# Two transposes taken from TensorE and done by VectorE in 32x32 blocks and by DMA through DRAM, in a fused local/pooled attention and maxout kernel

## The chip, the cores and the metric

The kernel runs on one core of a Trainium2 chip. The core has five engines that run at once: TensorE (PE in the profile), VectorE (DVE), ScalarE (ACT), GpSimd (POOL) and SyncE (SP, which here only issues DMA transfers). The metric is the device time of one execution in microseconds (us); lower is better.

## The reference

Two kinds of attention over 8 batches x 8 heads x 576 tokens x 64 dims are added, and the sum goes through a maxout layer. All is float32.

```python
q_d = q.reshape(B, H, Sd, factor, D).mean(axis=3)        # factor = 4, Sd = 144; k_d and v_d alike
out_up = np.repeat(sm_attn(q_d, k_d, v_d), factor, axis=2)   # pooled attention, full softmax over 144
mask = np.abs(pos[:, None] - pos[None, :]) < factor       # local attention: 7 neighbours
scores = np.where(mask, scale * np.matmul(q, k.transpose(0, 1, 3, 2)), -1000000000.0)
attn = softmax(scores)
x = (out_up + np.matmul(attn, v))                         # then (8 * 576, 512)
h = np.maximum(np.maximum(x @ w1, x @ w2), x @ w3)        # 512 -> 768
return h @ w_out                                          # 768 -> 512
```

## The kernel before, in words

The 4608 tokens are cut into nine blocks `j` of 512 tokens. Block `j` from 0 to 7 is the first 512 tokens of batch `j`; block 8 collects the last 64 tokens of all eight batches. In a block, token `4r + f` lies in partition `r` at position `f`, so that one partition holds a pooled group of four tokens. A block's attention runs in two halves `n = 2j` and `n = 2j + 1` of four heads each.

**Local attention of blocks 2 to 8.** `scores(n)` computes windows of scores on TensorE, writes them to DRAM (`scr`) and reads them back so that each token's seven scores lie in its partition (`s`). `values(n)` loads V with its neighbours (`v`, two buffers), multiplies it by the seven weights into `pvb` (on ACT, POOL or DVE) and adds up on DVE into `x`, a tile of 128 partitions (r) x 4 (f) x 128 (two heads x 64 dims). Each block has four such tiles, `c = 0..3`; tag `x` has five buffers. Blocks 0 and 1 take another path (`DENSE`, `band_values`) that leaves x already transposed.

**Pooled attention of blocks 0 to 7.** `pooled_scores(n)` multiplies pooled q and k on TensorE, takes maxima on DVE, exponentials on ACT (into `pd`, 128 x 2 x 2 x 144, and the tail's `pdt`, 64 x 144), and then needs the softmax with the key on the partition. Before, TensorE transposes it with the identity: four matmuls of `pd`, one of `pdt`, one of `ptl`, and a small one of `ptd` with `diag` that gathers the corner; copies bring the results from PSUM into `pt` and `ptt`. `pooled_values(n)` multiplies them by pooled V (`vd`, `vtail`) and ACT scales the result into `od`.

**The maxout layer** (`mlp_in`, `mlp_out`) needs x with the feature on the partition. `turn(j)` calls `transposes(j, c)`: before, four TensorE transposes of an x tile into one PSUM bank (`psx`), one DVE add of `od` into `xs` (tag `t`, three buffers), and a split into a high part `xhi` (ACT) and a low part `xlo`. The float32 product is made of three products of high and low parts, so a block costs 216 matmuls in `mlp_in` (tile names `xhi`, `xlo`, `whi`, `wlo`) and 72 in `mlp_out` (`hh`, `wo`), each 128x128 by 512 columns. `xhi` and `xlo` have one buffer for each `c`, so block `j + 1` can be split only when `mlp_in(j)` has read them.

**What sets the order.** The kernel's code only records operations. A planner in it (`Recorder.place`) gives each operation a cost, a priority and a readiness time, runs a list schedule with these costs and writes every engine's instructions in that order; where an operation has several forms (`either`, `copy`, `tt`) it also picks the engine. On the chip each engine then executes its list in order, and waits where an operand has not come. Transfers are all issued by SP in such a list. On PE, attention comes before the maxout layer whenever it is ready by the plan, and the maxout layer fills the rest. Since one helper emits everything, all instructions carry one line in the profile (L409); they are told apart by their tiles. PSUM has eight banks, four of tag `pm` for the maxout layer (and block 0), four of tag `pa`.

Of the kernel before, what the change touches and what calls it, by code (L numbers as in the profile page):

```python
# [28 lines left out]
HH = 4  # L29
# [7 lines left out]
SCR = HH * SEG * (KWIN + 1)  # L37
QKW = S + 6
# [73 lines left out]
class Recorder:  # L112
# [46 lines left out]
    def add(self, forms, bias={}):  # L159
# [20 lines left out]
        for write, aps in ((False, ins), (True, outs)):  # L180
            for ap in aps:
# [245 lines left out]
def local_global_attention_maxout_kernel(ctx: ExitStack, tc: tile.TileContext, qk_d, qke_d, vw_d, wi_d, wo_d, v, ident_d, mask_d, diag_d, band_d, out):  # L427
# [47 lines left out]
    pdt = new([P, SD], name="pdt")  # L475
# [37 lines left out]
    def load_constants():  # L513
        for t in (*qtail, *vtail, pdt, ptd, ptl, nm, zd):
            dve.memset(t, 0.0)
# [61 lines left out]
    def tail_pooled(n):  # L577
# [7 lines left out]
        vs = new([N64, D], tag="vs", name=f"vs_{n}")  # L585
# [3 lines left out]
    def pooled_scores(n):  # L589
# [15 lines left out]
        pd = new([P, 2, 2, SD], tag="pd", name=f"pd_{n}")  # L605
        for x in range(4):
            i, pr = x // 2, x % 2
            act.activation(pd[:, i, pr], sps[i][:, pr], AF.Exp, bias=nm[:, x : x + 1], scale=1.0 / 128.0, accum_out=zd[:, x : x + 1])
        act.activation(pdt[:N64], spt, AF.Exp, bias=nm[:N64, 4:5], scale=1.0 / 128.0, accum_out=zd[:N64, 4:5])
# [4 lines left out]
        dve.tensor_tensor(out=ptl[:, :N64].rearrange("p (r i x) -> p i r x", r=2, i=2), in0=pd[:, :, :, P:], in1=rb.broadcast_to([P, 2, 2, TAIL]), op=ALU.mult)  # L614
        kw = dict(out=pd[:, :, :, :P], in0=pd[:, :, :, :P], in1=rb.broadcast_to([P, 2, 2, P]), op=ALU.mult)
        muls = [("mul", (pd[:, x // 2, x % 2, :P], pd[:, x // 2, x % 2, :P], rd[:, x : x + 1]), {}) for x in range(4)]
        rec.add({"DVE": [("tensor_tensor", (), kw)], "ACT": muls})
        dve.tensor_scalar_mul(pdt[:N64], pdt[:N64], rd[:N64, 4:5])
        dve.tensor_tensor(out=ptd[:N64, :N64].rearrange("p (h x) -> p h x", h=HH), in0=pdt[:N64, P:].unsqueeze(1).broadcast_to([N64, HH, TAIL]), in1=diag[:N64, :HH].unsqueeze(2).broadcast_to([N64, HH, TAIL]), op=ALU.mult)
        pt = new([P, HH, SD], tag="pt", name=f"pt_{n}")  # L620
        ptt = new([P, SD], tag="ptt", name=f"ptt_{n}")
        pst1 = bank([P, HH, P], "pa", f"pt1_{n}")
        pst2 = bank([P, 2 * P + TAIL], "pa", f"pt2_{n}")
        with together():
            for g in range(HH):
                pe.transpose(pst1[:, g], pd[:, g % 2, g // 2, :P], ident)
            pe.transpose(pst2[:, :P], pdt[:, :P], ident)
            pe.transpose(pst2[:, P : 2 * P], ptl, ident)
            pe.matmul(pst2[:, 2 * P :], ptd, diag[:, HH:], start=True, stop=True, skip_group_check=True)
        copy(pt[:, :, :P], pst1)  # L630
        act.copy(pt[:, :, P:], pst2[:, :N64].rearrange("p (g x) -> p g x", g=HH))
        act.copy(ptt, pst2[:, P:])
        st["pt"], st["ptt"] = pt, ptt

    def pooled_values(n):
# [4 lines left out]
        vt, pt, ptt, vd = vtail[n % 2], st["pt"], st["ptt"], st["vd"]  # L640
        po = bank([P, 2, SD], "pa", f"po_{n}")
        with together():
            for pr in range(2):
                for last, (a, p) in enumerate(((vd, pt), (vt, ptt))):
                    for i in range(2):
                        g = 2 * pr + i
                        pe.matmul(po[64 * i : 64 * i + 64, pr], a[:, g], p if last else p[:, g], start=not last, stop=bool(last), tile_position=(0, 64 * i), skip_group_check=True)
# [44 lines left out]
    def values(n):  # L692
# [7 lines left out]
        for g in range(HH):  # L700
# [16 lines left out]
            rec.add({"POOL": pooladd, "DVE": pooladd})  # L717
        if j < B:
# [72 lines left out]

    def transposes(j, c):
# [152 lines left out]
```

## Time and profile before

| | |
|---|---|
| median of 3 runs | 755.56 us (753.48 to 756.48) |
| the profiled execution | 756.08 us, of which span 754.3 us |
| PE busy | 717.5 us (95%) |
| VectorE busy | 505.4 us (67%) |
| ScalarE busy | 409.9 us (54%) |
| GpSimd busy | 178.7 us (24%) |
| DMA queue of SP | 83885 packets, 76.34 MB, 35.9% of 16 engines' span |
| granted TensorE clock | 0.984 |

The span is the time from the first to the last instruction of the profiled execution. An engine's busy time is the time in which at least one of its instructions ran. The mean duration of a matmul overlaps that of the next one, so the pace of a run of matmuls is read from the distance of their starts. "Idle before" is the time for which an engine waited ahead of an instruction, and "<-" names what ended it.

### The profile page before, as it was taken

The page shows a single profiled execution, that of the slowest core. Times are in us where ns is not written, and L with a number is a line of the kernel's source. Part 1 is how long each engine was busy: PE and PEld are TensorE (multiplying, and loading weights), DVE is VectorE, ACT ScalarE, POOL GpSimd, SP SyncE. Part 2 cuts the span into 40 slices and gives each one's busy share as a digit, 9 for nine tenths or more (in the row PEclk, how much of TensorE's full clock was granted, in tenths as well). Part 3 has the DMA queues.
Part 4 walks back from the last instruction along what each step waited for, and adds up shares of the span by engine and source line. Part 5 has one row for each costly group of instructions (what it writes and reads, how often), then busy time and mean ns, then how long its engine had stood idle before and what let it go on. Part 6 is the DMA issues. An engine that isn't in the chain of part 4 may idle for free.

```text
span 754.3 us, 13132 instructions
## 1 busy us (share of the span) xinstructions
PE 717.5 (95%) x4752; PEld 580.3 (77%) x4752; DVE 505.4 (67%) x981; ACT 409.9 (54%) x1404; POOL 178.7 (24%) x243
## 2 busy tenths in 40 slices
PE   3669999999999999999999999999999999999997
PEld 2556777788788888788778878888888788888885
DVE  6998999638977887867954895489448727241220
ACT  4764666445948565676835774478437927121111
POOL 0003000024605442426303440245015405000000
PEclk9859999999999999999999999999999999999999
DMA  8935332652345252642245224532432231000002
GB/s 293 360 102 201 116 96 85 210 123 69 103 114 153 39 159 52 176 124 59 93 126 118 55 85 136 98 74 85 133 69 74 64 97 35 1 29 29 0 1 56
DMA packets 83951, 77.18 MB, mean 102 GB/s; under 512 B 61503, under 2 KB 64862, under 8 KB 83118
## 3 DMA queue, kind: packets, MB, share of 16 engines
q1 hardware_dynamic: 83885, 76.34, 35.9%
q8 instruction: 37, 0.61, 0.3%
q14 instruction: 29, 0.23, 0.1%
HBM read 58.86 MB, written 17.47 MB: 101 GB/s over the span
## 4 chain that ended last, share of the span: by engine, by line
PE 68%; DVE 4%; issue 0%; ACT 0%; DVEq 0%; ACTq 0%
PE pm L409 60%; PE pa L409 8%; DVE pvb L409 2%; DVE t L409 1%; DVE x L409 0%; DVE xlo_0r L409 0%; DVE hh_1r L409 0%; DVE hp L409 0%; DVE nm L409 0%; DVE pd L409 0%; ACT hh_0r L409 0%; DVE hv L409 0%; ACT y L409 0%; DVE qkT L409 0%; DVE qtail L409 0%
## 5 line engine op out<-in xcount | busy, mean ns | idle before, releaser
L409 PE MATMUL pm<-xlo_0r,whi_0r 128*128 128x512 f32 x648 | 254.5, 393 | 0.9 <-DVE xlo_0r L409 0.9
L409 PE MATMUL pm<-xhi_0r,wlo_0r 128*128 128x512 f32 x648 | 254.2, 392 | 0.2 <-DVE wlo_0r L409 0.2
L409 PE MATMUL pm<-xhi_0r,whi_0r 128*128 128x512 f32 x648 | 254.1, 393 | 0.0
L409 POOL TENSOR_TENSOR pvb<-v,s 128x256 f32<-128x256 f32 x205 | 152.1, 774 | 272.1 <-DVE s L409 145.7
L409 ACT ACTIVATE pvb<-v,s 128x64 f32<-128x64 f32 x748 | 187.2, 338 | 15.0 <-DVE s L409 6.3
L409 DVE TENSOR_TENSOR t<-pm,t 128x512 f32<-128x512 f32 x108 | 74.3, 688 | 130.2 <-PE pm L409 119.3
L409 PEld LDWEIGHTS pm<-xlo_0r,whi_0r 128*128 128x128 f32 x648 | 121.9, 188 | 27.2 <-DVE xlo_0r L409 1.6
L409 PEld LDWEIGHTS pm<-xhi_0r,wlo_0r 128*128 128x128 f32 x648 | 121.9, 188 | 26.2 <-DVE wlo_0r L409 0.6
L409 PEld LDWEIGHTS pm<-xhi_0r,whi_0r 128*128 128x128 f32 x648 | 122.1, 188 | 25.6 <-issue 0.5
L409 DVE TENSOR_TENSOR pvb<-pvb 128x768 f32<-128x768 f32 x112 | 107.1, 956 | 2.4
L409 ACT CAST hh_0r<-t 128x512 fp32r<-128x512 f32 x54 | 33.4, 619 | 96.5 <-DVE t L409 96.4
L409 PE MATMUL pm<-wo_1r,hh_0r 128*128 128x512 f32 x216 | 84.8, 393 | 0.0
L409 PE MATMUL pm<-wo_0r,hh_1r 128*128 128x512 f32 x216 | 84.7, 395 | 0.0
L409 PE MATMUL pm<-wo_0r,hh_0r 128*128 128x512 f32 x216 | 84.5, 395 | 0.0
L409 ACT COPY y<-pm 128x512 f32<-128x512 f32 (+1 forms) x44 | 25.4, 585 | 72.6 <-PE pm L409 62.0
L409 ACT COPY t<-pm 128x512 f32<-128x512 f32 x54 | 31.4, 582 | 32.2 <-PE pm L409 32.0
L409 DVE TENSOR_TENSOR hh_1r<-t,hh_0r 128x512 fp32r<-128x512 f32 x54 | 38.8, 718 | 13.8 <-ACT hh_0r L409 13.8
L409 PEld LDWEIGHTS pm<-wo_0r,hh_1r 128*128 128x128 f32 x216 | 40.5, 188 | 9.4 <-issue 1.1
L409 PEld LDWEIGHTS pm<-wo_1r,hh_0r 128*128 128x128 f32 x216 | 40.6, 188 | 9.2 <-issue 0.8
L409 PEld LDWEIGHTS pm<-wo_0r,hh_0r 128*128 128x128 f32 x216 | 40.4, 188 | 9.3 <-issue 0.4
L409 DVE COPY sm<-pa 128x280 f32<-128x280 f32 x31 | 13.5, 445 | 24.2 <-PE pa L409 22.6
L409 DVE TENSOR_TENSOR x<-pvb 128x256 f32<-128x256 f32 x56 | 28.2, 503 | 1.9
(121 smaller groups left out, 733.1 us busy)
## 6 DMA issues: line engine op xcount, KB each, us to landing
qk<-in_qk_dram SPq DMA_DIRECT2D x32, 582.0 KB
v<-in_v_dram SPq DMA_DIRECT2D x55, 320.0 KB
out_dram<-y SPq DMA_DIRECT2D x36, 256.0 KB
scr<-sm SPq DMA_DIRECT2D x56, 140.0 KB
wo<-in_wi_dram SPq DMA_DIRECT2D x4, 1536.0 KB
hh<-in_wi_dram SPq DMA_DIRECT2D x2, 1536.0 KB
pvb<-in_wo_dram SPq DMA_DIRECT2D x6, 512.0 KB
qk<-in_qke_dram SPq DMA_DIRECT2D x4, 582.0 KB
```

Source lines behind the costliest of these rows:

```text
L409: getattr(self.engines[o.eng], method)(*map(real, args), **{k: real(x) for k, x in kw.items()})
```

## The change

For the halves `n = 4` to `15`, the pooled softmax is no longer transposed on TensorE. `pd` gets 16 more columns for each head (zeroed by POOL), so that its 160 columns are five blocks of 32. VectorE transposes `pd` (128 x 640) and `pdt` (64 x 160) in place, in blocks of 32x32: each block is turned, but stays where it was. Eight DMAs write the blocks to their right places in a DRAM tile `pdd` (four of `pd` with runs of 32 elements, 128 bytes; four of `pdt` with runs of 16 elements), and three DMAs read `pt` and `ptt` back in whole rows.

For blocks 2 to 8, the new function `turned(j, c)` does the same with each x tile as soon as its two heads are done: one VectorE transpose (128 x 512) into another buffer of tag `x`, four DMAs with runs of 128 bytes into a DRAM tile `xd`, and in `transposes(j, c)` one DMA that reads `xs` back; `od` is then added in SBUF, on VectorE or GpSimd.

In all, 28 x tiles and 12 halves: TensorE loses 208 matmul instructions, VectorE gains 28 + 12 + 12 transposes, and SP's list grows from 258 to 530 DMAs. `ptl`, `ptd`, the PSUM copies into `pt` and `ptt`, and the PSUM banks of all these fall away there. `Recorder.add` no longer orders two writes to the same DRAM tile (they do not overlap). The weights' and the dense blocks' paths are kept.

```diff
@@ Recorder.add
-                    if (w or write) and q is not o and (info["psum"] or (a0 < p1 and p0 < a1 and (am & m))):
+                    if (w or write) and q is not o and (info["psum"] or (a0 < p1 and p0 < a1 and (am & m))) and not (w and write and info["tag"][0] == "DRAM"):
@@ pooled_scores
-        pd = new([P, 2, 2, SD], tag="pd", name=f"pd_{n}")
+        pd = new([P, 2, 2, SD5], tag="pd", name=f"pd_{n}")
+        gps.memset(pd[:, :, :, SD:], 0.0)
...
+        else:
+            dve.transpose(out=pd, in_=pd)
+            dve.transpose(out=pdt[:N64], in_=pdt[:N64])
+            d = rec.tile([SD5 * HH * SD], F32, "pdd", 2, f"pdd_{n}", "DRAM")
+            w = HH * SD
+            for a in range(P // 32):
+                src = pd[32 * a : 32 * a + 32].rearrange("p i r (b q) -> p (i r) b q", q=32)
+                sp.dma_start(dram(d, 32 * a, [[w, 32], [SD, HH], [32 * w, SD5 // 32], [1, 32]]), src)
             for g in range(HH):
-                pe.transpose(pst1[:, g], pd[:, g % 2, g // 2, :P], ident)
...
+                pr, i = g // 2, g % 2
+                src = pdt[32 * pr : 32 * pr + 32].rearrange("p (b h x) -> p b h x", h=2, x=TAIL)[:, :, i]
+                sp.dma_start(dram(d, (2 * i + pr) * SD + P, [[w, 32], [32 * w, SD5 // 32], [1, TAIL]]), src)
+            sp.dma_start(pt, dram(d, 0, [[w, P], [1, w]]))
+            for a in range(2):
+                sp.dma_start(ptt[32 * a : 32 * a + 32], dram(d, P * w + a * SD, [[2 * SD, 2], [w, TAIL], [1, SD]]))
@@ values, after the second head of an x tile
+            if g % 2:
+                turned(j, h // 2)
+    def turned(j, c):
+        blk = state["blk", j]
+        x = blk["x"][c].rearrange("p f i d -> p f (i d)")
+        t = new([P, FAC, P], tag="x", bufs=XBUFS, name=f"xt_{j}_{c}")
+        dve.transpose(out=t, in_=x)
+        d = blk["xd"][c] = rec.tile([P * FAC * P], F32, "xd", 2 * NCC, f"xd_{j}_{c}", "DRAM")
+        w = FAC * P
+        for a in range(P // 32):
+            src = t[32 * a : 32 * a + 32].rearrange("p f (b q) -> p f b q", q=32)
+            sp.dma_start(dram(d, 32 * a, [[w, 32], [P, FAC], [32 * w, P // 32], [1, 32]]), src)
@@ transposes
             xs = new([P, FAC * P], tag="t", bufs=3, name=f"xs_{j}_{c}")
+            sp.dma_start(xs, dram(blk["xd"][c], 0, [[FAC * P, P], [1, FAC * P]]))
...
-            x = blk["x"][c].rearrange("p f i d -> p f (i d)")
-            ps = bank([P, FAC, P], "pa", f"psx_{j}_{c}")
-            with together():
-                for f in range(FAC):
-                    pe.transpose(ps[:, f], x[:, f], ident)
-            dve.tensor_tensor(out=xs3, in0=ps, in1=od, op=ALU.add)
+            tt(xs3, xs3, od, ALU.add)
```

The planner makes a new order from this. Attention also ends earlier in PE's list: after its last matmul stand 893 matmuls of the maxout layer (29 of one block and three whole blocks of 288), where before 468 stood behind the last transpose. Three places show the new order. The first is PE's list where block 2's attention ends (half `n = 5`), inside `mlp_out(1)`: `pa<-pt,vd` are the pooled values, `pa<-ident,x` the transposes of the four x tiles, `pm<-wo,hh` the maxout layer. Before:

```order
L409 MATMUL pm_160<-wo_0r,hh_1r 128x512
L409 MATMUL pa_199<-pt_336,vd_437 64x144 x2
L409 MATMUL pa_199<-ptt_350,vtail_0_97 64x144 x2
L409 MATMUL pa_199<-pt_336,vd_437 64x144 x2
L409 MATMUL pa_199<-ptt_350,vtail_0_97 64x144 x2
L409 MATMUL pa_305<-ident_91,x_121 128x128 x4
L409 MATMUL pa_193<-ident_91,x_123 128x128 x4
L409 MATMUL pa_195<-ident_91,x_125 128x128 x4
L409 MATMUL pa_199<-ident_91,x_184 128x128 x4
L409 MATMUL pm_160<-wo_0r,hh_0r 128x512
```

The same place now, where `pa<-qkT` are the pooled scores of the next half:

```order
L410 MATMUL pm_166<-wo_0r,hh_0r 128x512
L410 MATMUL pa_199<-pt_339,vd_439 64x144 x2
L410 MATMUL pa_199<-ptt_109,vtail_0_99 64x144 x2
L410 MATMUL pa_199<-pt_339,vd_439 64x144 x2
L410 MATMUL pa_199<-ptt_109,vtail_0_99 64x144 x2
L410 MATMUL pa_203<-qkT_158 128x144
L410 MATMUL pa_307<-qkT_158 128x144
```

The sixteen transposes are gone, and the next half's pooled scores follow at once (before, five matmuls of the maxout layer stood between). The second place is SP's list around the softmax of half `n = 5`: `v`, `qk` and `s` are the local attention's loads, `t<-xd` the loads of `xs`, `out_dram<-y` the results. Before:

```order
L409 DMA v_129<-in_v_dram 128x640
L409 DMA v_131<-in_v_dram 128x640
L409 DMA scr_1331<-sm_156 64x8x70
L409 DMA out_dram<-y_262 128x512
L409 DMA scr_1331<-sm_189 64x8x70
L409 DMA traw_127<-in_v_dram 64x1x256
```

Now:

```order
L410 DMA v_133<-in_v_dram 128x640
L410 DMA t_396<-xd_1673 128x512
L410 DMA pdd_1953<-pd_91 128x5x32 x2
L410 DMA t_615<-xd_1756 128x512
L410 DMA pdd_1953<-pd_91 128x5x32 x2
L410 DMA pdd_1953<-pdt_101 32x5x16 x4
L410 DMA xd_2005<-x_125 128x4x32 x4
L410 DMA s_1466<-scr_1344 128x16x7
L410 DMA pt_339<-pdd_1953 128x576
L410 DMA ptt_109<-pdd_1953 32x1x144 x2
L410 DMA v_135<-in_v_dram 128x640
```

Between two loads of `v` there now stand eighteen other DMAs, among them the whole way of the softmax out and back. The third place is VectorE's list at the turn of block 2, where the last x tile gets `od` and is split (`xlo`). Before:

```order
L409 TENSOR_TENSOR t_391<-pa_195,od_369 128x512
L409 TENSOR_TENSOR xlo_0r<-t_394,xhi_0r 128x512
L409 TENSOR_TENSOR xlo_0r<-t_612,xhi_0r 128x512
L409 TENSOR_TENSOR t_394<-pa_199,od_369 128x512
L409 TENSOR_TENSOR hp_152<-qk_158 128x576
L409 TENSOR_TENSOR qkT_154<-hp_152 128x2x144
L409 TENSOR_TENSOR xlo_0r<-t_391,xhi_0r 128x512
```

Now:

```order
L410 TENSOR_TENSOR t_393<-t_393,od_371 128x512
L410 TENSOR_TENSOR pd_91<-pd_91,rd_269 128x4x144
L410 TENSOR_SCALAR pdt_101<-pdt_101,rd_269 64x144
L410 STREAM_TRANSPOSE pd_91<-pd_91 128x640
L410 STREAM_TRANSPOSE pdt_101<-pdt_101 64x160
L410 COPY sm_193<-pa_307 128x280
L410 COPY sm_193<-pa_197 128x280
L410 TENSOR_TENSOR xlo_0r<-t_393,xhi_0r 128x512
```

The add of `od` now takes an operand that a DMA has brought, and the next half's softmax with its two transposes stands between the add and the split.

More of the change, by code (lines that the diff above doesn't have):

```diff
@@ L37 @@
 SCR = HH * SEG * (KWIN + 1)
+SD5 = SD + TAIL
 QKW = S + 6
@@ L474, in local_global_attention_maxout_kernel @@
     vtail = [new([P, HH, D], name=f"vtail{i}") for i in range(2)]
-    pdt = new([P, SD], name="pdt")
+    pdt = new([P, SD5], name="pdt")
+    ptt = new([P, SD], name="ptt")
     ptd = new([P, P], name="ptd")
@@ L513, in load_constants @@
     def load_constants():
-        for t in (*qtail, *vtail, pdt, ptd, ptl, nm, zd):
+        for t in (*qtail, *vtail, pdt, ptd, ptl, ptt, nm, zd):
             dve.memset(t, 0.0)
@@ L618, in pooled_scores @@
[L618 to L623, printed above, removed]
@@ L624, in pooled_scores @@
-        with together():
-            for g in range(HH):
-                pe.transpose(pst1[:, g], pd[:, g % 2, g // 2, :P], ident)
[L627 to L632, printed above, removed]
@@ L633, in pooled_scores @@
-        st["pt"], st["ptt"] = pt, ptt
+        w = P if n in DENSE else SD
+        kw = dict(out=pd[:, :, :, :w], in0=pd[:, :, :, :w], in1=rb.broadcast_to([P, 2, 2, w]), op=ALU.mult)
+        muls = [("mul", (pd[:, x // 2, x % 2, :w], pd[:, x // 2, x % 2, :w], rd[:, x : x + 1]), {}) for x in range(4)]
+        if n in DENSE:
+            dve.tensor_tensor(out=ptl[:, :N64].rearrange("p (r i x) -> p i r x", r=2, i=2), in0=pd[:, :, :, P:SD], in1=rb.broadcast_to([P, 2, 2, TAIL]), op=ALU.mult)
+        rec.add({"DVE": [("tensor_tensor", (), kw)], "ACT": muls})
@@ new lines, in pooled_scores @@
+        dve.tensor_scalar_mul(pdt[:N64, :SD], pdt[:N64, :SD], rd[:N64, 4:5])
+        pt = st["pt"] = new([P, HH, SD], tag="pt", name=f"pt_{n}")
+        if n in DENSE:
+            dve.tensor_tensor(out=ptd[:N64, :N64].rearrange("p (h x) -> p h x", h=HH), in0=pdt[:N64, P:SD].unsqueeze(1).broadcast_to([N64, HH, TAIL]), in1=diag[:N64, :HH].unsqueeze(2).broadcast_to([N64, HH, TAIL]), op=ALU.mult)
+            pst1 = bank([P, HH, P], "pa", f"pt1_{n}")
+            pst2 = bank([P, 2 * P + TAIL], "pa", f"pt2_{n}")
+            with together():
+                for x in range(HH):
+                    pe.transpose(pst1[:, x], pd[:, x // 2, x % 2, :P], ident)
+                pe.transpose(pst2[:, :P], pdt[:, :P], ident)
+                pe.transpose(pst2[:, P : 2 * P], ptl, ident)
+                pe.matmul(pst2[:, 2 * P :], ptd, diag[:, HH:], start=True, stop=True, skip_group_check=True)
+            copy(pt[:, :, :P], pst1)
+            act.copy(pt[:, :, P:].rearrange("p (i r) x -> p r i x", i=2), pst2[:, :N64].rearrange("p (r i x) -> p r i x", r=2, i=2))
+            act.copy(ptt, pst2[:, P:])
+        else:
[6 more added lines that the diff above has]
+                sp.dma_start(dram(d, 32 * a, [[w, 32], [SD, HH], [32 * w, SD5 // 32], [1, 32]]), src)
+            for g in range(HH):
+                pr, i = g // 2, g % 2
[4 more added lines that the diff above has]
+                sp.dma_start(ptt[32 * a : 32 * a + 32], dram(d, P * w + a * SD, [[2 * SD, 2], [w, TAIL], [1, SD]]))
```

16 lines of the change are left out of this document (6 added, 10 removed).

## The prediction

> **What bounds the kernel now.** I read the page's head and its 40 slices first: which engine is full, and where.
>
> ```profile
> span 754.3 us, 13132 instructions
> PE 717.5 (95%) x4752; PEld 580.3 (77%) x4752; DVE 505.4 (67%) x981; ACT 409.9 (54%) x1404; POOL 178.7 (24%) x243
> PE   3669999999999999999999999999999999999997
> DVE  6998999638977887867954895489448727241220
> q1 hardware_dynamic: 83885, 76.34, 35.9%
> ```
>
> PE is full from the fifth slice on. A 9 hides up to a tenth, so I asked for busy times by stretches (columns: stretch, its length, busy us of PE, weight loads, DVE, ACT, POOL, then clock, DMA share, GB/s).
>
> ```profile
> 0.00:100.00 100.00, 71.43 (x702) 55.86 (x703) 89.28 (x165) 59.73 (x188) 9.15 (x14) 0.88 0.61 205
> 100.00:740.00 640.00, 637.36 (x4015) 517.50 (x4014) 416.13 (x817) 348.39 (x1213) 169.52 (x229) 1.00 0.33 87
> 360.00:380.00 20.00, 19.98 (x96) 15.93 (x94) 19.48 (x40) 15.23 (x55) 4.93 (x7) 1.00 0.24 83
> 380.00:400.00 20.00, 19.14 (x225) 15.09 (x223) 10.13 (x28) 6.81 (x24) 0.90 (x1) 1.00 0.44 119
> 0.00:528.00 528.00, 497.58 (x3563) 399.61 (x3564) 414.14 (x816) 327.13 (x1146) 145.86 (x198) 0.98 0.44 125
> ```
>
> Between 100 and 740 us PE is idle for 2.6 us in all (640 - 637.36), at full clock. So there the time is PE's work; the 28.6 us of idle before 100 us belong to the dense blocks, which keep their path. One microsecond less of PE work after 100 us is one microsecond less of span, as long as no other engine makes PE wait. The 380-to-400 row shows what such a wait looks like: after a stretch in which DVE was busy for 19.48 of 20 us, PE lost 0.86 us. The chain of waits in order of time ends with
>
> ```profile
> 642.62 106.12 PE pm L409 x468
> ```
>
> that is, 468 matmuls of the maxout layer without a break, 0.2268 us each. Attention is done 110 us before the end, so it sets nothing there.
>
> **The change part by part. PE.** Mean durations overlap, so the price of a transpose is the distance of starts in PE's timeline:
>
> ```profile
> 280.48 1.97 PE L409 MATMUL pa<-ident,x 128*128 128x128 f32 x16
> 282.20 0.47 PE L409 MATMUL pm<-xhi_0r,whi_0r 128*128 128x512 f32 x1
> 282.51 0.39 PE L409 MATMUL pm<-xlo_0r,whi_0r 128*128 128x512 f32 x1
> ...
> 302.43 0.60 PE L409 MATMUL pa<-ident,pd 128*128 128x128 f32 x4
> 302.87 0.27 PE L409 MATMUL pa<-ident,pdt 128*128 128x128 f32 x1
> 302.98 0.27 PE L409 MATMUL pa<-ident,ptl 128*128 128x128 f32 x1
> 303.09 0.29 PE L409 MATMUL pa<-diag,ptd 128*128 128x16 f32 x2
> 303.31 0.41 PE L409 MATMUL pa<-qk 64*64 64x70 f32 x11
> ```
>
> Sixteen x transposes take 282.20 - 280.48 = 1.72 us; there are 112 (first group below), so 12.0 us. The softmax of one half takes 303.31 - 302.43 = 0.88 us; twelve halves make 10.6 us. The last block's four groups stand alone in PE's list, and the first matmul after such a group costs 0.31 instead of 0.23 us, so 0.4 us more. Sum: 23.0 us less PE work.
>
> **VectorE.** No row shows a VectorE transpose. The nearest rows are operations of the same 512 columns:
>
> ```profile
> L409 PE MATMUL pa<-ident,x 128*128 128x128 f32 x112 | 14.2, 275 | 0.0
> L409 DVE TENSOR_TENSOR t<-pm,t 128x512 f32<-128x512 f32 x108 | 74.3, 688 | 130.2 <-PE pm L409 119.3 <-ACT pvb L409 8.5 <-ACT pd L409 1.6
> L409 DVE TENSOR_TENSOR hh_1r<-t,hh_0r 128x512 fp32r<-128x512 f32 x54 | 38.8, 718 | 13.8 <-ACT hh_0r L409 13.8
> L409 DVE TENSOR_TENSOR t<-pa,od 128x512 f32<-128x512 f32 x24 | 16.1, 682 | 0.1
> L409 ACT COPY pt<-pa 128x512 f32<-128x512 f32 x13 | 7.6, 583 | 14.9 <-PE pa L409 14.9
> L409 DVE COPY pt<-pa 128x512 f32<-128x512 f32 x3 | 2.1, 685 | 0.9 <-PE pa L409 0.9
> L409 DVE TENSOR_TENSOR ptd<-pdt,diag 64x64 f32<-64x64 f32 x16 | 4.4, 277 | 0.5
> L409 DVE TENSOR_TENSOR ptl<-pd,rd 128x64 f32<-128x64 f32 x16 | 4.0, 252 | 0.5
> L409 DVE TENSOR_SCALAR pvb<-pvb 128x512 f32<-128x512 f32 x6 | 2.5, 421 | 1.4 <-ACT pvb L409 1.3
> ```
>
> So 0.42 to 0.72 us for an x tile; I take 0.69, since the plain copy from PSUM costs that, and in proportion 0.85 for `pd` and 0.35 for `pdt`: 28 x 0.69 + 12 x 0.85 + 12 x 0.35 = 33.7 us (at 0.42 throughout in proportion, 21). Off go `ptl`, `ptd` and three copies, 12 x 0.53 + 2.1 = 8.4 us; the adds of `od` stay on VectorE at about 0.68. Net with small shifts, 26 us more: 531. ACT loses nine copies at 0.58 and 24 small ones, some 11 us, and was not the bound (54%); twelve small memsets go to POOL, which has 75% free: nothing.
>
> Is there room for 26 us? PE's new list has 893 maxout matmuls behind the last attention matmul, 893 x 0.2268 = 202.5 us, so attention must be through at 731 - 202.5 = 528 us. VectorE's work behind that is three blocks of maxout (12 maxima at 0.69, six splits at 0.72, four adds and splits of x: 18 us each) and the last heads, some 12 us; 531 - 67 = 464 us must fit into 528, or 88%. Before, the same 528 us held 414 us, 78%. It fits, but stretches like the 360-to-380 one, after which PE waits for 0.8 us, will be more frequent. Before, three waits of that size make up the 2.6 us; I go to about nine: 5 us more. Bounds: none (the planner spreads it better), and 15 us, when every other stretch of attention ends so.
>
> By the Trainium skill (VectorE: DVE Perf Modes, section on the three transpose paths) a 128x128 transpose takes 311 ns on VectorE and 390 on TensorE, for bf16. By that an x tile would be 1.24 us, all of it 58 instead of 34 us, VectorE at 92%; and PE's part would look worth 80 us, where this trace has 0.11 us from one transpose to the next.
>
> **DMA.** The nearest transfers are the scores' way through DRAM (`scr`: 512 runs of 280 bytes; `s`: 2048 runs of 28 bytes); the issues, two stretches with one of each in them beside result stores, and when the data was used:
>
> ```profile
> L409 SPq DMA_DIRECT2D scr<-sm x56: 574/591/3569, 138.6 to 610.1; - x56
> ...
> 610.00:613.00 3.00, 3.00 (x15) 2.46 (x15) 0.00 (x0) 0.00 (x0) 0.00 (x0) 1.00 0.49 138
> 614.40:616.20 1.80, 1.80 (x10) 1.49 (x9) 0.00 (x0) 0.00 (x0) 0.00 (x0) 1.00 0.41 146
> 616.20:618.20 2.00, 2.00 (x10) 1.66 (x9) 0.00 (x0) 0.59 (x1) 0.00 (x0) 1.00 0.56 28
> ...
> 610.12 0.58 SPq L409 DMA_DIRECT2D scr<-sm  x1
> 614.50 0.61 SPq L409 DMA_DIRECT2D s<-scr  x1
> ...
> 618.58 0.21 DVE L409 TENSOR_TENSOR s<-s,mask 128x48 f32<-128x48 f32 x1 [11.77 <-DMA s<-scr]
> ```
>
> The third stretch is mostly `s`: 1.12 us of 16 engines for 2048 packets, 9 ns each. The first holds a 256 KB store (0.74 us, the second stretch) and `scr`: 0.73 us for 512 packets, 23 ns. A run of 128 bytes lies between; I take 14. One x tile is then 2048 x 14 / 16 = 1.8 us, one softmax (3200 packets) 2.8; with the whole rows read back at the store's rate, 0.75 and 1.0 us: 28 x 2.55 + 12 x 3.8 = 117 us. DMA goes from 0.359 x 754 = 271 to 388 us of 731, 53%: hidden, as long as nothing waits for one transfer.
>
> SP issues 272 more: 208 scatters at 0.59 and 64 reads at some 0.35 make 145 us, over 430 us of attention. Its queue has that time: it stood waiting for the buffers of `v` alone for
>
> ```profile
> SPq L409 <- ACT pvb L409: 160.2, 46, 9.4
> ```
>
> But while it waits for a VectorE transpose, the loads of `v` behind it wait too.
>
> A round trip through DRAM is long: out 614.50 - 610.12 = 4.4 us, back 618.58 - 614.50 = 4.1. For x it is hidden: x tiles are stored as they are made, and from block 3 on the plan has 23 us and more of maxout work between attention's end and their use. Block 2 follows at once (11 us), and may cost 0 to 3 us; this is within the 5.
>
> **Sum.** 756.1 (the profiled execution's own time, span + 1.8) - 23.0 + 5 = 738.1 us, 2.4% less. The median of the runs is 0.5 below that execution, which changes nothing.
>
> **The rivals.** *Slower: the pooled softmax's loop.* PE's new list puts the scores of a half right behind the pooled values of the half before, so scores, softmax, round trip and values follow each other in a ring. The chain showed this once so: scores, transposes (the first eight of the 40), window scores, values (part of the 28).
>
> ```profile
> 288.82 1.06 PE pa L409 x12
> ...
> 302.60 1.43 PE pa L409 x40
> ...
> 305.62 0.65 PE pa L409 x32
> ...
> 314.89 2.19 PE pa L409 x28
> ```
>
> From the transposes' place the new way takes 1.2 (VectorE) + 8 x 0.59 (issues) + 3.8 + 3 x 0.35 + 4.1 = 14.9 us, where 12.3 lay between transposes and values here. Scores to transposes is 36 to 55 matmuls in PE's old list, 8 to 12.5 us. So the ring needs 23 to 27 us. PE's new list leaves 98 to 163 matmuls and two groups of window scores (0.65 us each, the x32 row): 23.5 to 38 us, with three of the twelve halves below 24. Queues in front of SP or VectorE come on top. PE cannot pass a waiting matmul, so each microsecond late is lost. It decides at 23 / 12 = 1.9 us late for each half; at 3.5 it gives 756.1 - 23 + 42 = 775. Against it: the plan allows for a trip, and most halves have 3 us to spare. 17%.
>
> *Smaller gain: VectorE becomes the bound.* If a transpose takes 1.1 us or POOL's work slows VectorE, occupancy passes 92% and waits come to 12 to 23 us: 745 to 756. For it: 19.48 of 20 us already occurs. 22%.
>
> *The DMA engines fill.* The Trainium skill warns (VectorE: DVE Perf Modes, section on the three transpose paths) that a copy that transposes by its strides is 19 times slower than the crossbar. At nineteen times the store's 0.74 us an x tile would take 14 us and a softmax 18, together 610 us beside the 271: 881 us. The 9 and 23 ns packets above speak against it, since every run here is 64 or 128 bytes long. 3%.
>
> *More than forecast.* x tiles are freed earlier, the waits of before vanish too: 729 to 731. 5%.
>
> **How the numbers follow.** My forecast, 731 to 745, has 53%. A measurement of this kernel can tell about 0.5%, 3.8 us, from no change. Faster by more than that: 53 + 5 + half of the smaller gain, 69%; within it: the other half and the mildest ring, 13%; slower: the rest of the ring and the DMA case, 18%. The range for 8 in 10 is 729 to 757.
>
> **What would show it.** Right: PE about 23 us less busy, the transposes at 0.6 to 0.8 us in VectorE's groups, PE idle of 5 to 10 us after 100 us, DMA near 50%. Wrong: PE waiting at `pa<-pt,vd` for a DMA (the ring), at `pm` for VectorE (the smaller gain), SP's queue waiting for its own transfers (the DMA case), or transposes above 1 us.

## The result, and the profile after

The changed kernel takes 774.32 us (median of 4 runs, 769.22 to 776.07), the kernel before 755.58 beside it: 1.0241 times as long, 95% interval 1.0216 to 1.0266. The sum of the prediction was 738.1 us, its range for 8 in 10 729 to 757. The kernel is slower where faster was forecast. The page of its profiled execution (busy us, share and instructions of each engine; then PE's busy tenths and its granted clock in 40 slices; then the DMA queue):

```profile
span 774.3 us, 13146 instructions
PE 706.7 (91%) x4544; PEld 562.9 (73%) x4544; DVE 532.7 (69%) x1008; ACT 389.0 (50%) x1331; POOL 187.0 (24%) x273
PE   3578999999998999899897989899999999999997
PEclk9869999999999999999899989999999999999999
q1 hardware_dynamic: 189533, 99.44, 52.4%
```

PE has 208 instructions less, and the 9s that filled its row before are broken by 8s and a 7 in slices 13 to 26. In slices 20 and 24 the granted clock drops too. Before, the stretch from 100 to 560 us read so (stretch, length, PE busy, clock, DMA share, GB/s):

```profile
100.00:560.00 460.00, 458.15 (x3143) 1.00 0.40 107
```

After, with five short stretches from its middle:

```profile
100.00:560.00 460.00, 430.58 (x2860) 0.97 0.66 149
...
360.00:380.00 20.00, 17.81 (x81) 1.00 0.90 173
380.00:400.00 20.00, 19.36 (x148) 0.83 0.55 152
400.00:420.00 20.00, 16.82 (x77) 1.00 0.88 166
420.00:440.00 20.00, 19.21 (x150) 0.91 0.54 88
440.00:460.00 20.00, 16.68 (x78) 0.83 0.69 162
```

PE's idle time there went from 1.9 to 29.4 us. At 380, 420 and 440 us a stretch with a lower clock follows one in which PE waited; in it PE counts as "busy" but is slower. PE's waits between 100 and 600 us (us in total, times, longest):

```profile
PE pa L410 <- DMA pt<-pdd: 9.9, 7, 2.9
PE pa L410 <- ACT pd L410: 7.4, 6, 2.8
PE pa L410 <- DMA ptt<-pdd: 7.1, 7, 2.3
PE pm L410 <- DVE hh_1r L410: 2.7, 3, 1.6
```

The pooled values wait for `pt` and `ptt` to come back from DRAM, 17.0 us in all. One such wait on SP's queue (start, duration):

```profile
410.78 2.59 SPq L410 DMA_DIRECT2D xd<-x  x4
...
414.16 1.33 SPq L410 DMA_DIRECT2D v<-in_v_dram  x1
415.58 0.38 SPq L410 DMA_DIRECT2D pt<-pdd  x1
416.01 1.38 SPq L410 DMA_DIRECT2D ptt<-pdd  x2
```

in the chain of waits:

```profile
416.74 3.91 DMA ptt<-pdd
420.65 0.14 issue
420.79 3.43 PE pa L410 x24
...
566.13 202.65 PE pm L410 x893
```

and on PE, with an earlier one (in brackets the idle time before the instruction):

```profile
378.34 0.50 PE L410 MATMUL pm<-wo_0r,hh_0r 128*128 128x512 f32 x1 [1.29 <-ACT hh_0r L410]
379.74 0.51 PE L410 MATMUL pa<-pt,vd 128*64 128x144 f32 x4 [0.90 <-DMA pt<-pdd]
380.89 0.75 PE L410 MATMUL pa<-ptt,vtail 128*64 128x144 f32 x4 [0.64 <-DMA ptt<-pdd]
...
419.22 0.47 PE L410 MATMUL pa<-pt,vd 128*64 128x144 f32 x4 [2.87 <-DMA pt<-pdd]
420.79 0.59 PE L410 MATMUL pa<-ptt,vtail 128*64 128x144 f32 x4 [1.10 <-DMA ptt<-pdd]
```

The load of `pt` is issued at 415.58 and its data used at 419.22, 3.6 us later; the second load of `ptt` is issued at 416.74, and its data is used at 420.79, 4.05 us later. The last line of the chain is the end: 893 maxout matmuls behind attention, as planned, but from 566 us on and not from 528.

**Where the 20.0 us of span went** (754.3 to 774.3). PE idle: 754.3 - 717.5 = 36.8 before, 774.3 - 706.7 = 67.6 after, 30.8 more. PE busy: 10.8 less. The same 4544 matmuls in a better order (late_130, below) are busy for 692.5, so 25.0 us of work did go, and 706.7 - 692.5 = 14.2 us came back as slower matmuls (most of it the clock, as the last section shows). 30.8 + 14.2 - 25.0 = 20.0.

### The profile page after: what moved, and what is told of

It is laid out like the page before. It is cut to its first block, busy times and chain, and to the rows that moved or that the text cites. A ratio compares the mean times of both kernels' runs of the same rounds, so it can differ in the third digit from the quotient of the medians.

```text
span 774.3 us, 13146 instructions
## 1 busy us (share of the span) xinstructions
PE 706.7 (91%) x4544; PEld 562.9 (73%) x4544; DVE 532.7 (69%) x1008; ACT 389.0 (50%) x1331; POOL 187.0 (24%) x273
## 3 DMA queue, kind: packets, MB, share of 16 engines
q1 hardware_dynamic: 189533, 99.44, 52.4%
## 4 chain that ended last, share of the span: by engine, by line
PE 42%; DVE 23%; DMA 16%; SPq 7%; ACT 6%; issue 4%; POOL 3%; DVEq 0%; ACTq 0%; POOLq 0%
PE pm L410 37%; SPq L410 7%; DVE pvb L410 6%; PE pa L410 5%; ACT pvb L410 3%; DVE t L410 3%; POOL pvb L410 3%; DMA s<-scr 2%; DMA ptt<-pdd 2%; DMA v<-in_v_dram 2%; DMA x<-in_vw_dram 2%; DVE x L410 2%; DMA scr<-sm 2%; DVE sm L410 1%; DVE xlo_0r L410 1%
## 5 line engine op out<-in xcount | busy, mean ns | idle before, releaser
L410 POOL TENSOR_TENSOR pvb<-v,s 128x256 f32<-128x256 f32 x214 | 155.4, 759 | 184.5 <-DVE s L410 85.6
L410 ACT ACTIVATE pvb<-v,s 128x64 f32<-128x64 f32 x712 | 179.0, 340 | 39.9 <-DMA v<-in_v_dram 24.6
L410 DVE TENSOR_TENSOR pvb<-pvb 128x768 f32<-128x768 f32 x112 | 103.5, 924 | 19.7 <-ACT pvb L410 12.3
L410 PEld LDWEIGHTS pa<-qk 64*64 64x64 f32 x1024 | 20.6, 138 | 20.5 <-ACT pd L410 9.4
L410 PE MATMUL pa<-qk 64*64 64x70 f32 x1024 | 26.4, 234 | 8.4 <-ACT pd L410 7.4
```

What stands on the lines that cost most here:

```text
L410: getattr(self.engines[o.eng], method)(*map(real, args), **{k: real(x) for k, x in kw.items()})
```

## The experiments

The change has two parts, and the planner orders everything anew. My first theory was the rival of the prediction, the ring through the pooled softmax; the others were that VectorE is too full, that SP's list is too long, and that the order as such is bad. PE busy, PE idle (span - busy) and clock are of the profiled execution. "Between" is the number of maxout matmuls that stand in PE's list between a half's pooled scores and its pooled values, mean of the halves 4 to 15, counted for the kernels of the planner series.

| run | median us | ratio to before, 95% | PE busy, idle | clock | between |
|---|---|---|---|---|---|
| before | 755.58 | | 717.5, 36.8 | 0.984 | 115 |
| after | 774.32 | 1.0241 (1.0216 to 1.0266) | 706.7, 67.6 | 0.970 | 118 |
| x_only | 750.71 | 0.9948 (0.9924 to 0.9971) | 702.3, 46.6 | 0.984 | |
| pooled_only | 762.49 | 1.0090 (1.0073 to 1.0107) | 709.4, 51.5 | 0.984 | |
| opened | 768.07 | 1.0153 (1.0102 to 1.0204) | 703.5, 61.6 | 0.978 | |
| planned | 738.74 | 0.9769 (0.9745 to 0.9794) | 692.7, 44.6 | 0.983 | 137 |
| before_planned | 760.29 | 1.0060 (1.0040 to 1.0081) | 718.4, 41.1 | 0.981 | |
| land_only | 745.57 | 0.9857 (0.9808 to 0.9907) | 698.3, 48.7 | 0.982 | 134 |
| issue_only | 758.55 | 1.0035 (1.0012 to 1.0059) | 702.2, 54.7 | 0.974 | 118 |
| land_short | 780.75 | 1.0348 (1.0303 to 1.0393) | 703.8, 73.2 | 0.973 | 112 |
| issue_532 | 768.47 | 1.0180 (1.0136 to 1.0224) | 704.5, 61.6 | 0.977 | 118 |
| land_new | 751.08 | 0.9941 (0.9919 to 0.9962) | 700.9, 49.7 | 0.980 | 135 |
| land_old | 749.12 | 0.9907 (0.9871 to 0.9943) | 697.3, 50.2 | 0.983 | 130 |
| free_pt | 764.72 | 1.0120 (1.0078 to 1.0162) | 705.4, 61.1 | 0.975 | 118 |
| lag_900 | 777.88 | 1.0287 (1.0246 to 1.0328) | 712.5, 63.7 | 0.966 | |
| x_planned | 756.93 | 1.0010 (0.9992 to 1.0028) | 707.9, 45.4 | 0.980 | |
| pooled_planned | 757.17 | 1.0025 (1.0005 to 1.0046) | 710.5, 46.3 | 0.981 | |
| land_long | 786.77 | 1.0406 (1.0385 to 1.0428) | 713.9, 70.6 | 0.952 | 144 |
| land_mid | 741.67 | 0.9813 (0.9796 to 0.9830) | 697.3, 42.5 | 0.980 | 143 |
| late_130 | 736.77 | 0.9760 (0.9735 to 0.9786) | 692.5, 40.0 | 0.985 | 133 |

### Each part alone

`x_only` keeps the pooled softmax on TensorE in all halves:

```diff
-        w = P if n in DENSE else SD
+        w = P
-        if n in DENSE:        # both places in pooled_scores
+        if True:
```

> Only the x tiles go by VectorE and DRAM; the pooled softmax is transposed on TensorE in all halves, as in the kernel before. Three theories. Ring (PE's list expects pt and ptt earlier than the round trip through DRAM brings them, and PE cannot pass the waiting pooled values): no pt from DRAM, so no such wait; PE saves 12.4 us and the time is 742 to 750. VectorE (its list is too full for the plan): it keeps 20 of the 34 us of transposes, so somewhat over half of the 43 us of loss stays, 756 - 12 + 24 = 768. SP (272 more DMAs hold up the loads of v): 140 of the 272 stay, half of the loss, 756 - 12 + 21 = 765.

`pooled_only` gives x back to TensorE:

```diff
-            if g % 2:
-                turned(j, h // 2)
-            sp.dma_start(xs, dram(blk["xd"][c], 0, [[FAC * P, P], [1, FAC * P]]))
...
-            tt(xs3, xs3, od, ALU.add)
...
+            with together():
+                for f in range(FAC):
+                    pe.transpose(ps[:, f], x[:, f], ident)
+            dve.tensor_tensor(out=xs3, in0=ps, in1=od, op=ALU.add)
```

> Only the pooled softmax goes by VectorE and DRAM; the x tiles are transposed on TensorE, as in the kernel before. Ring: all of the loss stays, perhaps a little less since no stores of x stand ahead of the load of pt; 756 - 10.6 + 30 to 40 = 775 to 785, and PE waits for pt and ptt for 15 us or more in all. VectorE: 14 of 34 us stay, 756 - 10.6 + 17 = 762. SP: 132 of 272 DMAs stay, 756 - 10.6 + 20 = 765.

x alone gains 5 us, the softmax alone loses 7, both together lose 19. x_only falls into the ring theory's 742 to 750 but for 0.7 us, and far from the other theories' 765 to 768: 28 transposes, 112 scatters and 28 reads by themselves cost less than they save. They are not free: PE is 15.2 us less busy, but 9.8 us more idle. pooled_only at 762.5 is far under that theory's 775 to 785: the ring alone isn't worth what the changed kernel lost. It fits VectorE's 762 and is near SP's 765, but its VectorE is busy for only 510.9 us (67%), and PE's waits between 100 and 600 us are small, of nine kinds; two of the three largest are:

```profile
PE pa L410 <- DMA pt<-pdd: 3.3, 4, 1.3
PE pa L410 <- DVE z L410: 2.0, 1, 2.0
```

### The ring opened, and the order drawn with other numbers

`opened` keeps both parts, but records the softmax of half n + 1 before the values of half n, and the loads of `pt` and `ptt` with the half that uses them:

```diff
         if j < B:
-            tail_pooled(n)
-            pooled_scores(n)
+            if "pdd" not in state[n]:
+                tail_pooled(n)
+                pooled_scores(n)             # now only up to the stores into pdd
+            pooled_load(n)                    # the three loads of pt and ptt
         if n < 2 * B + 1:
             with at(100.0 * n + 100.0, LAG):
                 begin(n + 1)
+                if (n + 1) // 2 < B:
+                    tail_pooled(n + 1)
+                    pooled_scores(n + 1)
         values(n)
```

> The changed kernel with the ring opened: the pooled scores and the softmax of half n + 1 are recorded ahead of the values of half n, and the load of pt and ptt stands by itself behind the pooled values of the half before. The same operations and the same DMAs in another order. Ring: the round trip gets a whole half of time, waits of PE for pt and ptt fall below 3 us in all, and the time is 733 to 745. VectorE and SP: the work and the transfers are the same, so 765 to 778.

`planned` is the changed kernel with three numbers of its planner changed:

```diff
-        return 530.0, False
+        return 600.0, False
...
-                dma_free = max(dma_free, t + 1200.0) + size / rate
-                o.end = lanes[lane] = dma_free + 1100.0
+                dma_free = max(dma_free, t + 2000.0) + size / rate
+                o.end = lanes[lane] = dma_free + 2000.0
```

> The changed kernel, with only the planner's numbers for a DMA changed: 4.0 us instead of 2.3 from issue to landing, and 0.60 instead of 0.53 us of SP for an issue. Operations, buffers and DMAs are the same; the lists come out with more maxout matmuls between pooled scores and pooled values. Ring: PE has work where it waited, 735 to 750. VectorE and SP: no order helps, 762 to 780.

With the ring opened the waits for `pt` and `ptt` vanish, and others stand in their place:

```profile
PE pa L410 <- ACT odtail L410: 12.0, 8, 3.3
PE pm L410 <- ACT hh_0r L410: 5.6, 3, 3.0
```

So the ring as a dependency is not by itself the cause: 768.1, where my theory had 733 to 745, and it fell here. `planned` gains 35.6 us on the changed kernel with the same operations and transfers. Its page and PE's waits between 100 and 600 us:

```profile
PE 692.7 (94%) x4544; PEld 556.4 (75%) x4544; DVE 530.9 (72%) x1000; ACT 394.2 (53%) x1342; POOL 201.9 (27%) x271
...
q1 hardware_dynamic: 189533, 99.44, 52.8%
```

```profile
PE pm L410 <- ACT wo_0r L410: 4.0, 2, 2.0
PE pa L410 <- DMA pt<-pdd: 2.2, 4, 0.9
PE pm L410 <- DVE wlo_0r L410: 1.0, 1, 1.0
```

VectorE and the DMA engines do as much as in the changed kernel (530.9 us, 52.8%), in less time, and PE waits for them for only 3.5 us in all (`pt` 2.2, `ptt` 0.3, `wlo` 1.0). This rules out both as the bound. The second theory, then: the planner counts on a transfer's data too early, and PE, which can't pass a waiting matmul, waits for what comes later.

### Is it these numbers, and is it the change that needs them?

`before_planned` is the kernel before with the three new numbers; `land_only` and `issue_only` change only the landing or only the issue in the changed kernel; `land_short` shortens the landing:

| run | on the kernel | issue, ns | landing, ns (ahead of the bytes, behind them) |
|---|---|---|---|
| before_planned | before | 530 to 600 | 1200 to 2000, 1100 to 2000 |
| land_only | after | 530 | 1200 to 2000, 1100 to 2000 |
| issue_only | after | 530 to 600 | 1200, 1100 |
| land_short | after | 530 | 1200 to 600, 1100 to 500 |

> The kernel before, with only the three numbers of its planner that run "planned" changed (a DMA's landing 2000 + 2000 ns where it had 1200 + 1100, its issue 600 ns where it had 530). If the gain of "planned" comes from data that the changed kernel newly brings by DMA on TensorE's path, the kernel before gains little: 748 to 758 us. If these numbers are simply a better order for any version of this kernel, it gains about as much as the changed one did (774 to 739, 35 us), as far as TensorE's 717 us of work allows: 728 to 740 us, and the comparison of "planned" with before was unfair. If the order is a lottery, anything from 745 to 770.

> The changed kernel with only the planner's landing time of a DMA lengthened (2000 + 2000 ns where it had 1200 + 1100); SP's issue stays at 530 ns. If the order failed because the planner took DMA data as there 2 us too early: 735 to 748 us, most of the gain of "planned" (738.7). If it failed because SP's list is longer in time than planned (the queue of issues, 272 more of them): 765 to 778.

> The changed kernel with only the planner's cost of an issue on SP raised from 530 to 600 ns; landing stays at 1200 + 1100 ns. If the landing time is the cause: 765 to 778 us, as the changed kernel (774.3). If SP's list is the cause: 735 to 750.

> The changed kernel with the planner's landing time of a DMA shortened to 600 + 500 ns (issue 530). A dose in the other direction: if the time comes from data that lands later than the plan says, TensorE waits more than in the changed kernel (29.4 us idle between 100 and 560 us): 785 to 810 us. If the changed kernel's order was only an unlucky draw and any other order is near 740 to 760, this one lies there too.

The kernel before gains nothing by them; it loses 0.6%. So these numbers don't simply make a better order for any version, and the comparison with before is fair. Of the 35.6 us the landing alone brings 28.7 and the issue alone 15.8 (758.6, between its two cases), so the two overlap. The shorter landing costs 6.4, less than the 10.7 or more expected, and no more than the scatter found below. The column "between" moves with the landing: 112, 118, 134. It is the time that the plan leaves for softmax and round trip: 118 x 0.2268 = 26.8 us in the changed kernel, 137 x 0.2268 = 31.1 in "planned". issue_only gained with its 118 unchanged, so this number isn't all; what else its order did well I haven't isolated.

The chain of "planned" says what a landing is on the chip, from the start of the issue to the end of PE's wait, where the chain runs through one:

```profile
210.27 5.59 DMA pt<-pdd
...
316.43 4.68 DMA pt<-pdd
388.81 6.56 DMA pt<-pdd
```

The planner gave a load of `pt` 3.2 us from the start of its issue (1.2 + 0.9 for its bytes + 1.1) and one of `ptt` 2.4, and more only where its transfers queue up. By the Trainium skill (DMA: Bandwidth & Descriptors, Anatomy of one DMA) a DMA has a fixed part of about 2.0 us and then its bytes at 436 GB/s; it says this for transfers that GpSimd issues. By that `pt`, 295 KB, would take 2.7 us, an estimate; the trace shows 4.7 to 6.6, with other transfers in flight. In the changed kernel the same view has 2.5 to 4.5 us for `ptt` and 4.8 to 6.6 for `v` between 100 and 600 us; for a load of `v` the plan's formula gives 3.3.

### A redraw, and whose landing

`issue_532` sets the issue to 532 ns. `land_new` adds 1700 ns to the landing of the change's own transfers only (pdd, xd), `land_old` to that of all others only. `free_pt` keeps the changed kernel's order on all engines, but sends the loads of `pt` and `ptt` elsewhere:

```diff
 issue_532:
-        return 530.0, False
+        return 532.0, False
...
 land_new, land_old:
+                new = any(i["tag"][1] in ("pdd", "xd") for i in o.tiles)
-                o.end = lanes[lane] = dma_free + 1100.0
+                o.end = lanes[lane] = dma_free + (2800.0 if new else 1100.0)    # land_old: 1100.0 if new else 2800.0
 free_pt, where the instructions are written out:
+                    to = ...                                                # the tag of the tile that is written
+                    if to in ("pt", "ptt") and method == "dma_start":
+                        ...
+                        self.engines["SP"].dma_start(dst, real(args[1]))        # dst: a place in DRAM
+                        continue
```

> The changed kernel with the planner's issue cost at 532 ns instead of 530: the order is drawn anew in many places, but its margins are the same. If the order counts by its margins: 765 to 780 us, within some 6 us of the changed kernel (774.3). If it is a lottery in which any redraw moves the time, so that "planned" and "issue_only" were lucky: anywhere from 738 to 785, and this run gives the size of the lottery.

> The changed kernel; the planner takes 1700 ns more until data is there, for the change's own transfers alone (those of pdd and xd); v, scr, s, qk stay at 1200 + 1100 ns. If the order failed on the change's own round trips: 740 to 755 us, as "land_only" (745.6). If it failed on the old loads that now stand behind 272 more issues: 762 to 778.

> The changed kernel; the planner takes 1700 ns more for every transfer except the change's own (so for v, scr, s, qk, results), while pdd and xd stay at 1200 + 1100 ns. If the change's own round trips are the cause: 762 to 778 us. If the old loads are: 740 to 755.

> The changed kernel's own order on every engine, all its transfers and matmuls; only, the three loads of pt and ptt of a half go to a place in DRAM instead, and the pooled matmuls read what halves 2 and 3 left in pt and ptt (so their values are not those of the half). TensorE then cannot wait for pt or ptt, which is 17 us of its 29 us idle between 100 and 560 us in the changed kernel. If these waits and the lower clock behind them are what the time went to: 748 to 760 us. If something else holds TensorE as much (pd on ScalarE, hh on VectorE, v loads) and takes their place: 765 to 775.

issue_532 turned out to be hardly a redraw: by its trace PE's, ScalarE's, GpSimd's and SP's lists are as they were, and on VectorE two pairs of neighbours change places. It came out 6 us faster than the changed kernel, in another group of runs: that is the size below which I read nothing into a single order. So it doesn't answer the lottery; the pattern of the real redraws of the changed kernel has to. The six whose plan has a landing of 4 to 5 us for some or all transfers (planned, land_only, land_new, land_old, land_mid, late_130) lie at 737 to 751, the three that leave it or shorten it at the old issue (opened, land_short, lag_900) at 768 to 781, and issue_only at 758.6 between them.

land_new (751.1) and land_old (749.1) each give most of land_only's gain (745.6), where I expected one to give it and the other nothing. That fits transfers of both kinds that are late, and a margin on either that loosens the rest too; it doesn't show which. free_pt gains 9.6 us of the 19, but only 3.8 beside issue_532 of the same group, with the same list on PE (768.5), and then waits one step earlier, for the exponentials that free the PSUM banks of the scores:

```profile
PE pa L421 <- ACT pd L421: 15.6, 10, 2.9
```

Its 764.7 is just outside either case (748 to 760, 765 to 775) and between them. Attention as a whole runs behind its plan there, and the wait for `pt` is the place where it first shows.

### Any slack, each part with the margin, and too much of it

`lag_900` leaves the transfers' numbers and gives every step of attention more slack; `x_planned` and `pooled_planned` are the two single parts with the three numbers of "planned"; `land_long` goes on to 3000 + 3000:

```diff
 lag_900:
-LAG = 600.0
+LAG = 900.0
 land_long (issue 600.0):
-                dma_free = max(dma_free, t + 1200.0) + size / rate
-                o.end = lanes[lane] = dma_free + 1100.0
+                dma_free = max(dma_free, t + 3000.0) + size / rate
+                o.end = lanes[lane] = dma_free + 3000.0
```

> The changed kernel with the planner's DMA numbers as they were, but 900 ns instead of 600 ns of slack after every operation of attention before another engine may take its result. If TensorE waits because attention in general runs later than planned, slack of any kind cures it: 736 to 752 us. If it must be where the transfers are, the slack on all the other steps only makes the chains longer: 758 to 775.

> Only x by VectorE and DRAM, the pooled softmax on TensorE (as "x_only", 750.7), with the planner's landing 2000 + 2000 and issue 600 ns. By the prediction's terms TensorE loses 12 us here; if the rest of its forecast (waits of about 2 us) holds with a margin: 742 to 747. If x_only's 5 us were all there is to have from x: 749 to 755.

> Only the pooled softmax by VectorE and DRAM, x on TensorE (as "pooled_only", 762.5), with the planner's landing 2000 + 2000 and issue 600 ns. By the prediction's terms TensorE loses 10.6 us here: 744 to 750 if the margin was all that it lacked. If the ring through the softmax costs by itself: 757 to 765.

> The changed kernel with a still longer landing, 3000 + 3000 ns (issue 600). If margin is all that counts and TensorE has other work for the time: 735 to 741 us, as "planned" (738.7), whose TensorE is idle for only 8 us between 100 and 560 us. If too much margin pushes attention back and the maxout layer runs out of blocks: 742 to 760.

Slack of any kind doesn't do: 777.9, beyond even the worse case. lag_900 still waits 15.8 us for `pt` and `ptt`, and leaves 119 matmuls between scores and values, as the changed kernel does. With a single part the margin didn't bring the forecast gain: 756.9 and 757.2, no faster than before. PE's work fell by 9.6 and 7.0 us (717.5 to 707.9 and 710.5), but its idle time rose by 8.6 and 9.5. "planned" has about as much (7.8 more than before), so with these numbers it looks like one price per order and not one per part. x_only, without the margin, is idle for as long (46.6 us) and faster all the same, since it is busy for 5.6 us less with the same matmuls, at a clock of 0.984 against 0.980. In x_planned the clock stands at 0.50 from 146.7 to 153.5 and from 201.3 to 204.7 us, with 9.45 us of PE's busy time in them, so 4.7 of the 5.6 us are lost there; x_only has no such stretch between 60 and 740 us. Ahead of the first, PE had waited for 3.6 us for a part of the weights (`wo_0r`).

land_long missed on the high side (786.8, expected 735 to 760), and PE's waits between 100 and 600 us say why:

```profile
PE pm L410 <- ACT xhi_0r L410: 24.8, 6, 8.8
PE pm L410 <- DVE xlo_0r L410: 6.4, 5, 2.7
```

and the end of its chain of waits:

```profile
642.05 136.96 PE pm L410 x603
```

PE waits no more for attention but, in the maxout layer, for the next block's split x, which attention has not delivered: a block's maxout is 288 matmuls and a block has two halves, so 144 between scores and values is all that there is, and land_long uses 144. (land_mid, below, uses 143 and waits there for only 4.7 us, so the count says that the room is used up, and not what more lag then costs.) Attention then ends at 642 us with 603 matmuls behind it; in "planned" it ended at 570.41 with 711. So the order has two sides: too little room and PE waits for `pt`, too much and it waits for `xhi`.

### Between the two, and the start

`land_mid` takes 2500 + 2500 (issue 600). `late_130` takes the numbers of "planned" only for transfers that the plan starts after 130 us, since "planned" lost PE time where the weights come in:

```diff
+                late = t > 130000.0
+                if late:
+                    free[e] = t + c + 70.0
+                dma_free = max(dma_free, t + (2000.0 if late else 1200.0)) + size / rate
+                o.end = lanes[lane] = dma_free + (2000.0 if late else 1100.0)
```

> The changed kernel with a landing of 2500 + 2500 ns and issue 600 ns in the planner, between "planned" (2000 + 2000: 738.7) and "land_long" (3000 + 3000: 786.8). If the time has its least near the chip's own landing of some 4 us and rises on both sides: 742 to 770. If 2000 + 2000 was one lucky draw and the rest is scatter: 765 to 790. If land_long was an unlucky draw: 735 to 742.

> As "planned" (landing 2000 + 2000, issue 600 ns), but only for transfers that the plan starts after 130 us; before, the planner's old numbers (1200 + 1100, 530), so that the weights come in as in the changed kernel. "planned" was busy for 74.4 of the 80 us from 100 to 180 us, the changed kernel for 78.8. If these 4.4 us can be had back with the rest kept: 731 to 737 us, the fastest so far. If the order's scatter (some 6 us, by issue_532) hides it: 735 to 750.

With the issue at 600 ns the landing in the plan gives, at 2.3, 4.0, 5.0 and 6.0 us: 758.6, 738.7, 741.7 and 786.8 us. That is flat from 4 to 5, near what the chip's landings are, and higher on both sides. 741.7 lies 0.3 us below the first case of land_mid and inside its last, by which land_long was an unlucky draw. PE's waits between 100 and 600 us in land_mid speak for the first:

```profile
PE pm L410 <- DVE xlo_0r L410: 2.9, 2, 2.2
...
PE pm L410 <- ACT xhi_0r L410: 1.8, 1, 1.8
```

It waits no more for `pt` (2.2 us in "planned") and already for the split x, where land_long waits for 31.2 us. With one order at each value the height at 6.0 is still that of a single order. late_130 is the fastest kernel here, 736.77, 0.9760 times before (0.9735 to 0.9786); "planned" is within the scatter of it. Its stretches and PE's waits:

```profile
100.00:180.00 80.00, 79.12 (x575) 1.00 0.51 132
180.00:560.00 380.00, 377.19 (x2467) 1.00 0.67 156
```

```profile
PE pm L413 <- DVE hh_1r L413: 1.5, 3, 0.6
PE pm L413 <- DVE wlo_0r L413: 0.7, 1, 0.7
PE pa L413 <- DMA ptt<-pdd: 0.6, 1, 0.6
```

PE is idle for 3.7 us between 100 and 560 us (0.9 + 2.8), at full clock. Between 100 and 180 us it is busy for 79.1 of 80, where "planned" had 74.4; so the weights' loads were what the longer landing had cost there.

## Why the prediction was wrong, point by point

**PE's work, 23.0 us less: right.** 717.5 to 692.5 us (25.0) in late_130, 692.7 in "planned", where waits and clock don't blur it. In the changed kernel only 10.8 of it is seen.

**VectorE, 531 us and room for it: right.** 532.7, with the new transposes

```profile
L410 DVE STREAM_TRANSPOSE x<-x 128x512 f32<-128x512 f32 x28 | 19.6, 699 | 0.3
...
L410 DVE STREAM_TRANSPOSE pd<-pd 128x640 f32<-128x640 f32 x12 | 10.0, 834 | 0.2
...
L410 DVE STREAM_TRANSPOSE pdt<-pdt 64x160 f32<-64x160 f32 x12 | 3.9, 321 | 0.2
```

at 0.70, 0.83 and 0.32 us (forecast 0.69, 0.85, 0.35). late_130 does as much in 732.5 us. "VectorE becomes the bound" did not happen.

**DMA, 53%: right as a share.** 52.4%, but of a longer span: 406 us where I had 388, so 135 us more and not 117. Nothing showed the 19-fold price.

**Waits, 5 us: the step that failed.** Where the sum has 5, the runs show 45.0: PE was idle for 30.8 us more, and slower matmuls took 14.2. I had counted only VectorE's busy stretches as a source of waits, at the size of "three waits" of 0.86 us before (the trace has two of 0.9 and 0.8 and three of 0.2 to 0.4), and left the round trip to the plan ("the plan allows for a trip, and most halves have 3 us to spare"). The plan allowed 2.4 to 3.2 us for the way back, while the same text had 4.4 out and 4.1 back from the trace of before, and I held these only against the room in PE's list (the ring rival), not against the planner's own number. With that number raised ("planned") PE's work is 24.8 us less and its idle time 7.8 us more, and the time is 738.7: the terms of the sum were near for that order, not for the one that the change got.

**The slower rival: right in place, its size met by luck, and only in part the cause.** At 3.5 us late for each half it gave 775, beside 774.3, and PE did wait at `pa<-pt,vd`. But the waits for `pt` and `ptt` are 17 us, 1.4 for each half and not 3.5, so that the two times meet is luck. Taking these waits away gave back 9.6 (free_pt; 3.8 beside issue_532), opening the ring 6.3 (opened), all near the scatter of 6. The rest was attention late in other places, and the clock. My estimate that the ring needs 23 to 27 us was short: in the eight halves that waited in the changed kernel, 25.8 to 35.2 us lie between the last pooled scores and the first pooled values. Orders that leave 26.8 us of maxout work on average wait, and those that leave 30 to 32 (133 to 143 matmuls) hardly do; to compare with my 23.5 to 38, 1.3 us of window scores have to be added to these.

**The clock: not in the sum at all.** Stretches behind waits ran at 0.83 and 0.91. Slower matmuls are 14.2 us, a third of the 45.0 us that the change lost. The clock stood at half in five spells between 100 and 560 us, with 22.6 us of PE's busy time in them (last section); that is 11.3 of the 14.2, and the rest isn't isolated. late_130 had no such spell there.

**SP's queue.** Its slack shrank as forecast: its waits for the buffers of `v` went from 160.2 us to

```profile
SPq L410 <- ACT pvb L410: 45.0, 30, 6.4
```

That a waiting entry holds back those behind it, which the prediction names, is not what stands at 414.16 above: the load of `v` ahead of `pt` takes 1.33 us, where the median of these issues is 0.41, but the waits of the queue have none for it; it is a slow issue. How much of the loss such entries make is open: I found no experiment that takes them away without moving the rest.

## What to carry to other kernels

Where a planner sets the order, a change that puts data on a new path must be costed by the planner's own number for that path: compare it with the landing in the trace before counting the work saved. TensorE, which runs its list in order, can pay for its waits twice, once as idle time (30.8 us here) and once as a lower clock behind them (11.3); so look at the clock beside the busy time, and not at busy time alone. And a margin has two ends: count the work that the engine has to fill it with (here 144 matmuls for each half), since past that the wait only changes its place.

## What the hardware showed that I had not expected

No single wait of PE between 100 and 600 us in the changed kernel lasted above 2.9 us, yet the 20 us behind two waits of 2.87 and 1.10 us read 0.91, and those behind the waits at 378 to 381 us (1.29, 0.90, 0.64) read 0.83. At 0.83, 3.4 us of 20 are lost; that is more than the waits themselves (2.8). Shorter stretches show how (stretch, length, PE busy, clock, DMA share, GB/s):

```profile
376.60:380.00 3.40, 1.21 (x7) 1.00 0.69 115
380.00:386.80 6.80, 6.16 (x34) 0.50 0.66 165
...
417.60:421.00 3.40, 0.68 (x8) 1.00 0.87 237
421.00:424.40 3.40, 3.40 (x25) 0.50 0.21 34
```

The clock stands at half for 6.8 or 3.4 us, and in the 3.4 us ahead PE was busy for 1.21 and 0.68 us, in pieces. Three more spells at half clock (from 195.7, 451.7 and 533.6 us) follow 3.4 us in which it was busy for 0.68, 0.66 and 1.83 us; the 3.4 us from 298.1 on, busy for 1.76, are followed by full clock. So it is how little PE did in some 3.4 us that goes with the drop, and not the longest wait; that the bound is near half is my estimate from these six, and they don't fix it.

By the Trainium skill (TensorE: Matmul & The Clock Gate, Part 1: The HAM clock gate) TensorE drops to half its clock after an idle window of about 3.4 us and comes back after as long a busy one. A loss of 3.4 us is two such windows at half clock, an estimate, and the 6.8 us at 0.50 bear it out; but no single wait here was as long as a window, and a few small matmuls ran between them.

The other surprise is the landing of transfers, 4.7 to 6.6 us for `pt` in "planned" with the DMA engines at 53% on the mean, where the prediction had 4.1 from a single load of `s` late in the kernel before, at 614.5 us.
